# Second feed-forward product of nine of twelve tile pairs by Strassen's scheme, with a new order of all tasks

## Chip, cores and metric

One core of a Trainium2 chip runs the whole program. The metric is the device time of one execution in microseconds (us); the time of a kernel is the median of several runs. The core has five engines with a queue of their own each: TensorE (PE; its weight loads, PEld, run beside its matmuls), VectorE (DVE), ScalarE (ACT), GpSimd (POOL) and SyncE (SP), which here only issues transfers.

## The reference

```python
def _attn_ref(q, k, v, f_logit):                 # (4, 8, 768, 48) each
    f = 1.0 / (1.0 + np.exp(-f_logit))
    for t in range(S):
        state = f[:, :, t, :, None] * state + np.einsum('bhd,bhe->bhde', k[:, :, t], v[:, :, t])
        y[:, :, t] = np.einsum('bhd,bhde->bhe', q[:, :, t], state)
def _moe_ref(x, w_in, w_out):                    # x (3072, 384), w_in (384, 2048), w_out (2048, 384)
    h = x @ w_in
    g = h * (1.0 / (1.0 + np.exp(-h)))
    return (g @ w_out).astype(np.float32)
```

A gated linear attention runs over 768 steps for 4 batches of 8 heads; its output, 3072 tokens of 384, goes through a feed-forward layer with SiLU. Inputs and output are float32; the kernel multiplies in bfloat16 with sums in float32.

## The kernel before

The 768 steps of each batch are cut into six chunks of 128 tokens, so there are 24 units (batch, chunk), taken two at a time as twelve pairs `P` = 0 to 11 (`PAIRS`). Pairs 0 to 3 (form `T`) hold the first two chunks of one batch, interleaved; the others (form `N`) hold the same chunk of two batches. The two units of a pair are numbered 0 and 1.

A unit is a row of tasks, each named by its kind, its pair and more numbers. The first half is the attention: `E`, `L` (ACT: logarithm of the gate), `cs` (PE: cumulative sums), `ia`, `a`, `al` (ACT: their exponentials), `ki`, `qg` (k and q scaled, on DVE or POOL), their transpose by PE (`tq`, copied out by `qkc`) or by a transfer (`qkD`), `sc` (PE: scores), `at` (DVE: masked scores), `y`, `yi` (PE: output), `d` (PE), `sd` (DVE) and `su` (POOL or DVE) for the state, `yc`, then `yT` with `xc`, or the transfer `yD`, for the transposed output `xT`. `vb` converts v.

The second half is the feed-forward layer. `mi.P.j` (L271) multiplies two of sixteen 128-wide column blocks of `w_in` with the 256 tokens of the pair. `si.P.j` (ACT, L276) applies SiLU and leaves `hT`, the hidden values with the hidden dimension on the partitions: 16 blocks n of 128 x 256 tokens. The second product is `mo.P.i.r` (L306): for unit i, four blocks n, each one weight load of 128 x 128 from `hT` and one matmul with 384 columns of `w_out`; four such tasks sum one unit in one PSUM bank. `oc` (L185 or L187) copies the sum to `ob`, `so` (L316, L318) stores it.

Nothing is scheduled at run time. A table `PLAN` lists all tasks in one order, with the engine of each (A, V, G, S, P for ACT, DVE, POOL, SP, PE) and the buffer it takes; each engine executes its own tasks in the order of the table and waits on semaphores for what it needs. The words `idle.512.n` are n matmuls on zeros (L465) that fill PE's time at the start. PSUM has eight banks (`pb`) for everything.

Of the kernel before, what the change touches and what calls it, by code (L numbers as in the profile page):

```python
# [33 lines left out]
SLOTS = dict(f=4, k=6, q=6, v=6, e=2, lf=3, x=5, qk=5, vb=7, qkT=4, qkTT=2, atm=4, yb=3, xT=4, hT=4, sd=2, al=6, ob=6, pb=8, st0=1, st1=1, st2=1, st3=1)  # L34
# [3 lines left out]
f.2.0:S:0 k.0.0:S:0 f.0.1:S:1 f.0.0:S: E.2.0:A:0 f.1.0:S:2 L.2.0:A:0 v.1.0:S:0 q.0.0:S:0 idle.512.11::0 cs.2.1:P:0 E.0.1:A:1 E.0.0:A: k.1.0:S:1  # L38
cs.2.0:P:1 L.0.1:A:1 L.0.0:A: E.1.0:A:0 q.1.0:S:1 idle.512.1::2 cs.0.0:P:2 cs.0.1:P:3 a.0.0:A:0 vb.1.1:G:0 f.3.0:S:3 L.1.0:A:2 ia.0.1:A:1 cs.1.0:P:4
a.0.1:A:2 qg.0.0:V:0 v.0.0:S:1 cs.1.1:P:5 ia.1.0:A:3 ki.0.1:V:1 al.1:A:0 ia.0.0:A:4 qg.0.1:V: al.0:A:1 ia.1.1:A:0 k.2.0:S:2 ki.0.0:V: vb.1.0:A:1  # L40
idle.512.4::6 tq.0.1:P:6 ki.1.0:G:2 ia.2.0:A:1 tq.0.0:P:7 qkc.0.1:V:0 a.1.0:A:2 q.2.0:S:2 qkc.0.0:A: qg.1.0:V: ki.1.1:V:3 a.1.1:A:4 idle.512.3::2
tq.1.0:P:2 q.3.0:S:3 a.2.0:A:3 qg.1.1:G: sc.0.0:P:3,4 qkc.1.0:A:1 sc.0.1:P:6,7 at.0.0.1:V:0 k.3.0:S:3 wi.1:G: at.0.0.0:V: E.3.0:A:1 idle.512.2::5
tq.1.1:P:5 at.0.1.0:V:1 wi.2:G: d.1:P:1,4 qkc.1.1:A: v.2.0:S:2 su.1.0:V:0 wi.0:G: at.0.1.1:V: al.2:A:2 L.3.0:A:0 idle.512.3::2 sc.1.0:P:2,3 ki.2.0:G:4
sc.1.1:P:6,1 at.1.0.1:V:2 vb.0.0:A:2 cs.3.1:P:5 vb.0.1:A:3 at.1.1.0:V:3 qg.2.0:G: al.3:A:3 ia.2.1:A:2 d.0:P:7,3 at.1.1.1:V: a.2.1:A:0 cs.3.0:P:6
ia.3.1:A:4 su.0.0:V:0 qg.2.1:G:2 y.0:P:0,1 a.3.0:A:1 at.1.0.0:V: yc.0.0:A:0 yi.0.1:P: tq.2.0:P:7 a.3.1:A:3 wi.3:G: yc.0.1:V:1 ia.3.0:A:0 y.1:P:0,2
wo.0:G: ki.2.1:V: yc.1.0:A:2 yT.0.0:P:5 sd.0.1:V:0 yi.1.1:P: yT.0.1:P:1 yc.1.1:A:0 tq.2.1:P:6 xc.0.0:V:0 wo.1:G: xc.0.1:A: qkc.2.0:V:0 v.3.0:S:3
yT.1.0:P:0 yT.1.1:P:3 xc.1.0:A:1 mi.0.2.0:P:2 qkc.2.1:V: su.0.1:G:0 xc.1.1:A: mi.0.3.0:P:5 mi.1.3.0:P:1 sd.1.1:V:1 mi.1.3.1:P: qg.3.0:V:3 wo.2:G:
# [24 lines left out]
qg.6.1:V: al.7.1:A:5 y.5.0:P:2 qkD.6.1:S:0 a.7.1:A:0 cs.8.1:P:5 yc.5.0:A:2 tq.6.0:P:3 ia.7.1:A:3 d.6.0:P:1 qkc.6.0:V:1 vb.7.1:A:3 cs.8.0:P:2
yD.5.0:S:1 mo.4.0.1:P: ia.8.0:A:1 ki.7.1:V:4 ia.8.1:A:2 sc.6.0:P:4,3 qg.7.1:V: al.8.0:A:1 a.8.0:A:4 mo.4.0.2:P: qkD.7.0:S:2 a.8.1:A:3 at.6.0.1:V:0
# [473 lines left out]
```

## Time and profile before

| | |
|---|---|
| runs | 181.47, 181.71, 182.23 us; median 181.71 us |
| span of the profiled execution, first to last instruction | 179.2 us |
| PE matmuls, weight loads | 170.5 us busy (95%), 129.0 us (72%) |
| DVE, ACT, POOL | 79.7 us (44%), 132.7 us (74%), 61.6 us (34%) |
| DMA | 31.91 MB, 178 GB/s in the mean |

The page gives no device time of the profiled execution beside its span; the median of the runs lies 2.5 us above this span, which is taken as the time around it. Busy time is the union of the spans of an engine's instructions, and a matmul's mean duration (326 ns with 384 columns) is its latency; the rate of a run of matmuls is read from when they start. In the chain of waits a piece is the work that the end of the program waited for, with its start and its length.

### The profile page before, as it was taken

The numbers are of one execution on the slowest core, as the hardware profiler recorded it, in microseconds if no ns is written. First come the engines' busy times: TensorE is split into PE (matmuls) and PEld (weight loads), VectorE is DVE, ScalarE is ACT, GpSimd is POOL, SyncE is SP. The second block draws the span as 40 slices with busy tenths as digits, with TensorE's granted clock in tenths as the row PEclk, the third lists the DMA queues.
The fourth block names the chain that finished last, engine by engine and source line by source line (L and its number), as shares of the span: only waits on it lengthen the run. The fifth ranks groups of instructions, "written<-read, shape, count | busy, mean of one in ns | idle before, by whom it ended". The sixth has DMA issues, their size and how long they took to land.

```text
span 179.2 us, 4981 instructions
## 1 busy us (share of the span) xinstructions
PE 170.5 (95%) x2042; PEld 129.0 (72%) x2044; DVE 79.7 (44%) x166; ACT 132.7 (74%) x251; POOL 61.6 (34%) x106
## 2 busy tenths in 40 slices
PE   6769989999999999999999999999999999999993
PEld 2345779975788866778678877875876786788782
DVE  7078994008821246456673703342335747500002
ACT  3989983895289999999967558988796991178410
POOL 6036995000274004554044170636303592000010
PEclk9999999999999999999999999999999999999999
DMA  6999999999999799998478998994994496320043
GB/s 159 324 325 325 240 204 207 199 187 190 242 230 212 92 208 221 168 241 144 84 145 170 188 210 141 252 263 103 179 251 94 97 190 215 88 70 0 0 150 117
DMA packets 109366, 31.91 MB, mean 178 GB/s; under 512 B 103536, under 2 KB 108768, under 8 KB 109344
## 3 DMA queue, kind: packets, MB, share of 16 engines
q1 hardware_dynamic: 104464, 25.60, 70.2%
q0 software_dynamic: 4880, 6.00, 15.7%
q8 instruction: 16, 0.26, 0.6%
q14 instruction: 6, 0.05, 0.1%
HBM read 25.17 MB, written 4.72 MB: 167 GB/s over the span
## 4 chain that ended last, share of the span: by engine, by line
PE 77%; ACT 9%; DVE 4%; DMA 3%; SPq 2%; issue 1%; POOL 1%; DVEq 0%
PE pb L306 32%; PE pb L271 32%; ACT hT L276 4%; DMA q<-in_q_dram 3%; PE pb L373 2%; SPq L241 2%; PE pb L385 2%; PE pb L348 2%; PE pb L389 2%; DVE qk L341 2%; ACT L513 1%; DVE atm L377 1%; PE pb L331 1%; PE pb L397 1%; DVE st L420 1%
## 5 line engine op out<-in xcount | busy, mean ns | idle before, releaser
L306 PE MATMUL pb<-w_out_sb,hT 128*128 128x384 bf16 (+1 forms) x416 | 70.4, 314 | 0.2 <-ACT hT L276 0.2
L271 PE MATMUL pb<-xT,w_in_sb 128*128 128x256 bf16 (+1 forms) x672 | 68.9, 257 | 0.0
L271 PEld LDWEIGHTS <-w_in_sb 128*128 128x128 bf16 x672 | 56.6, 98 | 7.5 <-issue 0.3
L276 ACT ACTIVATE hT<-pb 128x512 bf16<-128x512 f32 x96 | 51.8, 617 | 12.4 <-PE pb L271 12.0
L306 PEld LDWEIGHTS <-hT 128*128 128x128 bf16 x416 | 37.7, 98 | 18.7 <-ACT hT L276 0.4
L377 DVE TENSOR_TENSOR atm<-pb,triu 128x512 bf16<-128x512 f32 x32 | 20.6, 684 | 20.5 <-PE pb L373 17.8
L336 ACT ACTIVATE x<-pb 128x384 f32<-128x384 f32 x48 | 22.1, 508 | 1.5 <-PE pb L331 1.4
L420 POOL TENSOR_TENSOR st<-sd,al 48x192 bf16<-48x192 f32 x32 | 16.6, 518 | 18.7 <-PE pb L385 12.1
L341 POOL TENSOR_TENSOR qk<-q,x 128x384 bf16<-128x384 f32 x11 | 11.3, 1025 | 31.9 <-ACT x L336 14.5
L513 ACT ACT_TABLE_LOAD x15 | 19.2, 1283 | 0.3
L185 ACT COPY ob<-pb 128x384 f32<-128x384 f32 (+1 forms) x15 | 6.8, 453 | 12.6 <-PE pb L306 12.6
L377 DVE TENSOR_TENSOR atm<-pb,mask 128x512 bf16<-128x512 f32 x16 | 10.2, 685 | 12.4 <-ACT hT L276 11.1
L187 DVE COPY ob<-pb 128x384 f32<-128x384 f32 (+1 forms) x11 | 5.8, 535 | 22.2 <-PE pb L306 22.2
L318 POOL DMA_DIRECT2D out_dram<-ob x8 | 4.6, 578 | 28.4 <-ACT ob L185 24.8
L316 POOL DMA_DIRECT2D out_dram<-ob x14 | 7.6, 548 | 19.6 <-DVE ob L187 15.9
L341 DVE TENSOR_TENSOR qk<-q,x 128x384 bf16<-128x384 f32 x13 | 7.6, 593 | 13.7 <-ACT x L336 13.7
L248 ACT ACTIVATE e<-f 128x768 f32<-128x768 f32 (+1 forms) x13 | 10.4, 800 | 4.4 <-DMA f<-in_f_logit_dram 4.2
L410 DVE TENSOR_TENSOR sd<-pb,st 128x384 f32<-128x384 f32 x16 | 8.9, 554 | 10.6 <-PE pb L406 3.9
L341 POOL TENSOR_TENSOR qk<-k,x 128x384 bf16<-128x384 f32 x10 | 10.8, 1082 | 6.4 <-ACT al L278 2.0
L185 ACT CAST yb<-pb 128x384 bf16<-128x384 f32 x12 | 5.6, 479 | 9.7 <-PE pb L389 9.6
L341 DVE TENSOR_TENSOR qk<-k,x 128x384 bf16<-128x384 f32 x14 | 9.9, 710 | 0.9 <-ACT x L336 0.9
L187 DVE CAST yb<-pb 128x384 bf16<-128x384 f32 x12 | 6.6, 556 | 8.0 <-PE pb L389 5.9
(72 smaller groups left out, 157.4 us busy)
## 6 DMA issues: line engine op xcount, KB each, us to landing
f<-in_f_logit_dram SPq DMA_DIRECT2D x11, 384.0 KB, 4.7
q<-in_q_dram SPq DMA_DIRECT2D x16, 192.0 KB, 4.1
v<-in_v_dram SPq DMA_DIRECT2D x16, 192.0 KB, 3.9
k<-in_k_dram SPq DMA_DIRECT2D x16, 192.0 KB, 3.9
k<-in_k_dram SPq DMA_DIRECT2D x4, 384.0 KB, 4.8
v<-in_v_dram SPq DMA_DIRECT2D x4, 384.0 KB, 9.5
q<-in_q_dram SPq DMA_DIRECT2D x4, 384.0 KB, 4.9
w_in_sb<-in_moe_w_in_dram POOLq DMA_DIRECT2D x4, 384.0 KB, 9.5
```

The source lines that it names most:

```text
L185: nc.scalar.copy(dst, src)
L187: ENG[eng].tensor_copy(dst, src)
L248: return nc.scalar.activation(e, at("f", P)[:, j * w:(j + 1) * w], AF.Exp, scale=-1.0)
L271: nc.tensor.matmul(h[:, i, cols], w_in_sb[:, kk, n * 128:(n + 1) * 128], at("xT", P)[:, kk, cols], start=(kk == 0), stop=(kk == KT - 1))
L276: return nc.scalar.activation(at("hT", P)[:, 2 * j:2 * j + 2, :], at("h", P, j).rearrange("p (n c) -> p n c", n=2), AF.Silu)
L306: nc.tensor.matmul(at("o", P, i)[:, cols], at("hT", P)[:, n, i * C:(i + 1) * C], w_out_sb[:, n, cols], start=(n == 0), stop=(n == NT - 1))
L336: nc.scalar.activation(at(kind, P, i).rearrange("p h d -> p (h d)"), at("cs", P, i)[:, 0:HD], AF.Exp, scale=1.0 if kind == "ia" else -1.0)
L341: ENG[eng].tensor_mul(at("qk", P, i)[:, j, :, 0:D], heads("qk"[j], P, i), at("ia" if j else "a", P, i))
L377: ENG[eng].tensor_mul(at("atm", P, i)[:, r], at(f"s{r}", P, i).rearrange("p (n c) -> p n c", c=C), mask[:, None, :].to_broadcast([C, NP, C]))
L410: nc.vector.tensor_add(at("sd", P, i), d_ps, prev_state(P, i))
L420: ENG[eng].tensor_mul(at("st", P, i)[lo:lo + D, :, r * D:(r + 1) * D], src[lo:lo + D, :, r * D:(r + 1) * D], al_of(P, i)[lo:lo + D, :, Non ...
L513: nc.scalar.preload_act_table_set(TABLES[mode])
```

## The change

For pairs 2 to 10 the second product is done in blocks. Let A be the 256 tokens x 2048 hidden values, cut into the two units u and two halves k of the hidden dimension (eight blocks n each), and B be `w_out`, cut into two halves r of its rows and two halves c of its columns. In place of 32 matmuls with 384 columns there are seven products `ms.P.1` to `ms.P.7` of eight matmuls with 192 columns each:

M1 = (A00+A11)(B00+B11), M2 = (A10+A11)B00, M3 = A00(B01-B11), M4 = A11(B10-B00), M5 = (A00+A01)B11, M6 = (A10-A00)(B00+B01), M7 = (A01-A11)(B10+B11).

The sums of B are made once by five instructions `wt` on DVE. The sums of A are made for each pair by four instructions `hs` on DVE, bfloat16 in and out: `hs.P.5` with 2048 elements to a partition into a buffer of class `qkTT`, `hs.P.1` with 1024 into one of class `qkT`, `hs.P.6` and `hs.P.7` with 1024 in place in `hT`. One bank (`oa`) sums M3, M5 in one half and M4, M2 in the other. After M3 and M4 alone, `cc` (copy) and `ca.P.0` (DVE) take them into a buffer `ct`; only then may M2 and M5 be added in that bank. `ca.P.1` adds M1, `ca.P.2` and `ca.P.3` form the two diagonal blocks of the output and `oc.P` copies the two others. All of `ca` is on DVE.

`hT` gets the order (unit, n, token), the output buffer holds both units, E writes over `f`, and there are fewer buffers for f, k, q, v and `ob`. Pairs 0, 1 and 11 keep `mo`. The table is another one throughout: the pairs start in the order 1, 0, 2, 3 in place of 2, 0, 1, 3, there are 33 `idle` matmuls in place of 24, twelve `tq` in place of ten, and 25 of the store instructions are issued by SP in place of 12.

```diff
-SLOTS = dict(f=4, k=6, q=6, v=6, e=2, lf=3, x=5, qk=5, vb=7, qkT=4, qkTT=2, atm=4, yb=3, xT=4, hT=4, sd=2, al=6, ob=6, pb=8, st0=1, ...)
+SLOTS = dict(f=3, k=5, q=5, v=5, lf=3, x=5, qk=5, vb=7, qkT=5, qkTT=2, atm=4, yb=3, xT=4, hT=4, sd=2, al=6, ob=3, pb=8, st0=1, ..., ct=2)
...
-f.2.0:S:0 k.0.0:S:0 f.0.1:S:1 f.0.0:S: E.2.0:A:0 f.1.0:S:2 L.2.0:A:0 v.1.0:S:0 q.0.0:S:0 idle.512.11::0 cs.2.1:P:0 E.0.1:A:1 E.0.0:A: k.1.0:S:1
+f.1.0:S:0 q.1.0:S:0 f.0.0:S:1 f.0.1:S: f.2.0:S:2 k.1.0:S:0 E.1.0:A: L.1.0:A:0 E.0.0:A: f.3.0:S:0 idle.512.7::0 cs.1.0:P:0 ia.1.0:A:0 k.0.0:S:1
...
+    KH, W = NT // 2, d_model // 2
+    w_sum = {m: sb.tile([128, KH, W], BF16, name=f"w_sum{m}") for m in (1, 3, 4, 6, 7)}
...
+    BANK = {2: "oa", 3: "oa", 4: "oa", 5: "oa", 6: "ob2", 7: "ob2", 1: "oc"}
+    def h_sum(P, m):
+        if m == 5:
+            return at("hE", P).rearrange("p i j n g c -> p (i j n g c)").rearrange("p (u n c) -> p u n c", u=2, c=C)
+        if m == 1:
+            return at("hF", P).rearrange("p j n c -> p (j n) c")
+        return at("hT", P)[:, 1, 0:KH, :] if m == 6 else at("hT", P)[:, 0, KH:NT, :]
...
+        if kind == "wt":
+            blk = lambda r, c: w_out_sb[:, r * KH:(r + 1) * KH, c * W:(c + 1) * W]
+            x, y, op = {1: (blk(0, 0), blk(1, 1), ALU.add), 3: (blk(0, 1), blk(1, 1), ALU.subtract), ...}[rest[0]]
+            return ENG[eng].tensor_tensor(out=w_sum[rest[0]], in0=x, in1=y, op=op)
...
+        if kind == "hs":
+            x, y, op = {6: (blk(1, 0), blk(0, 0), ALU.subtract), 7: (blk(0, 1), blk(1, 1), ALU.subtract), 1: (blk(0, 0), blk(1, 1), ALU.add),
+                        5: (hT[:, :, 0:KH, :], hT[:, :, KH:NT, :], ALU.add)}[m]
+            return ENG[eng].tensor_tensor(out=h_sum(P, m), in0=x, in1=y, op=op)
+        if kind == "ms":
+            for n in range(KH):
...
+                half = 1 if m in (2, 4, 6) else 0
+                first = n == 0 and m in (1, 3, 6, 7)
+                nc.tensor.matmul(at(BANK[m], P)[:, half * W:(half + 1) * W], x, w, start=first, stop=(n == KH - 1), skip_group_check=True)
+            return
+        if kind == "cc":
+            return copy(eng, at("ct", P), at("oa", P)[:, W:2 * W])
+        if kind == "ca":
+            if rest[1] < 2:
+                return nc.vector.tensor_add(ct, at("oa", P)[:, 0:W] if rest[1] == 0 else at("oc", P)[:, 0:W], ct)
+            diag = at("ob", P).rearrange("p u (x w) -> p (u x) w", w=W)[:, 0:4:3, :]
+            if rest[1] == 2:
+                return nc.vector.tensor_sub(diag, ct[:, None, :].to_broadcast([C, 2, W]), two(at("oa", P)))
+            return nc.vector.tensor_add(diag, two(at("ob2", P)), diag)
...
-                e = at("e", P)[:, j * w:(j + 1) * w]
+                e = at("f", P)[:, j * w:(j + 1) * w]
...
-            return nc.scalar.activation(at("hT", P)[:, 2 * j:2 * j + 2, :], at("h", P, j).rearrange("p (n c) -> p n c", n=2), AF.Silu)
+            return nc.scalar.activation(at("hT", P).rearrange("p u n c -> p n u c")[:, 2 * j:2 * j + 2], at("h", P, j).rearrange("p (n u c) -> p n u c", n=2, u=2), AF.Silu)
...
-                nc.tensor.matmul(at("o", P, i)[:, cols], at("hT", P)[:, n, i * C:(i + 1) * C], w_out_sb[:, n, cols], start=(n == 0), stop=(n == NT - 1))
+                nc.tensor.matmul(at("o", P, i)[:, cols], at("hT", P)[:, i, n], w_out_sb[:, n, cols], start=(n == 0), stop=(n == NT - 1))
```

What the change moves is shown at three places, each engine's instructions in their order, with the numbers of the buffers behind the names. In PE's program, before, late in the kernel: the end of a task of the second product (384 columns to a matmul), then the first product of the next pair.

```order
3898 L306 MATMUL pb_140<-w_out_sb,hT_125 128x384
3899 L306 LDWEIGHTS hT_125
3900 L306 MATMUL pb_140<-w_out_sb,hT_125 128x384
3901 L271 LDWEIGHTS w_in_sb
3902 L271 MATMUL pb_141<-xT_121,w_in_sb 128x256
```

PE's program now, near its end: the end of M5 of pair 10 (the sum of A, in buffer `qkTT_104`, as the weights, 192 columns of `w_out_sb`), then half a task of pair 11 by the old way.

```order
4488 L273 MATMUL pb_135<-w_out_sb,qkTT_104 128x192
4489 L273 LDWEIGHTS qkTT_104
4490 L273 MATMUL pb_135<-w_out_sb,qkTT_104 128x192
4491 L370 LDWEIGHTS hT_120
4492 L370 MATMUL pb_134<-w_out_sb,hT_120 128x192
```

Each matmul keeps a weight load of its own, and there are more and narrower ones. In DVE's program in the middle of the kernel, before: masked scores (L377), state sums (L410), scaled q and k (L341).

```order
92 L410 TENSOR_TENSOR sd_127<-pb_140,st_151 128x384
93 L377 TENSOR_TENSOR atm_113<-pb_146,triu 128x512
94 L187 CAST yb_116<-pb_146 128x384
95 L341 TENSOR_TENSOR qk_96<-k_70,x_90 128x8x48
96 L377 TENSOR_TENSOR atm_114<-pb_143,triu 128x512
97 L377 TENSOR_TENSOR atm_114<-pb_141,triu 128x512
98 L341 TENSOR_TENSOR qk_94<-q_71,x_92 128x8x48
```

DVE's program now, at a like place: between the same kinds stand the assembly of pair 3 (L284, L285) and the sums of A of pair 4 (L256), with two operands in SBUF.

```order
120 L284 TENSOR_TENSOR ob_129<-ct_145,pb_134 128x2x192
121 L193 CAST yb_111<-pb_137 128x384
122 L285 TENSOR_TENSOR ob_129<-pb_133,ob_129 128x2x192
123 L193 COPY xT_115<-pb_139 128x3x128
124 L442 TENSOR_TENSOR atm_108<-pb_132,triu 128x512
125 L442 TENSOR_TENSOR atm_108<-pb_133,triu 128x512
126 L256 TENSOR_TENSOR qkT_101<-hT_118 128x1024
127 L193 CAST vb_94<-v_77 128x384
128 L256 TENSOR_TENSOR qkTT_104<-hT_118 128x2048
129 L442 TENSOR_TENSOR atm_109<-pb_138,triu 128x512
```

Scores that stood close together now wait behind sums of up to 2048 elements. DVE's end, before: the last masked scores, then only copies of sums to the output buffer.

```order
153 L377 TENSOR_TENSOR atm_114<-pb_145,triu 128x512
154 L377 TENSOR_TENSOR atm_113<-pb_146,triu 128x512
155 L187 COPY ob_134<-pb_142 128x384
156 L187 CAST yb_116<-pb_144 128x384
157 L187 COPY ob_139<-pb_145 128x384
158 L187 COPY ob_137<-pb_140 128x384
159 L187 COPY ob_134<-pb_146 128x192
```

DVE's end now: the sums of A and the assembly of pair 10 (`ct_144`, `hT_117`), with the copies of pair 11 (`ob_130`) between.

```order
223 L281 TENSOR_TENSOR ct_144<-pb_135,ct_144 128x192
224 L256 TENSOR_TENSOR hT_117<-hT_117 128x1024
225 L193 COPY ob_130<-pb_136 128x192
226 L281 TENSOR_TENSOR ct_144<-pb_132,ct_144 128x192
227 L193 COPY ob_131<-pb_135 128x384
228 L284 TENSOR_TENSOR ob_131<-ct_144,pb_135 128x2x192
229 L285 TENSOR_TENSOR ob_131<-pb_137,ob_131 128x2x192
230 L193 COPY ob_130<-pb_134 128x192
```

The last two additions of pair 10 stand ahead of DVE's last copy.

More of the change, by code (lines that the diff above doesn't have):

```diff
@@ L40 @@
[L40 to L47, printed above, removed]
@@ L425, in takes @@
     def takes(kind, rest):
-        if kind in ("wi", "wo", "so", "yi", "idle"):
+        if kind in ("wi", "wo", "wt", "so", "yi", "yj", "idle"):
             return []
```

209 lines of the change are left out of this document (131 added, 78 removed).

## Prediction

> **What bounds the kernel now.** I read the page's busy times and slices first, to see whether one engine is full:
>
> ```profile
> span 179.2 us, 4981 instructions
> PE 170.5 (95%) x2042; PEld 129.0 (72%) x2044; DVE 79.7 (44%) x166; ACT 132.7 (74%) x251; POOL 61.6 (34%) x106
> PE   6769989999999999999999999999999999999993
> PEclk9999999999999999999999999999999999999999
> GB/s 159 324 325 325 240 204 207 199 187 190 242 230 212 92 208 221 168 241 144 84 145 170 188 210 141 252 263 103 179 251 94 97 190 215 88 70 0 0 150 117
> ```
>
> then the busy time by stretches (PE, PEld, DVE, ACT, POOL with counts, granted clock, DMA):
>
> ```profile
> 0.00:27.00 27.00, 21.69 (x360) 13.94 (x362) 18.72 (x54) 22.76 (x45) 16.29 (x35) 1.00 1.09 263
> 27.00:176.00 149.00, 148.66 (x1688) 115.09 (x1682) 60.98 (x112) 109.64 (x205) 45.28 (x72) 1.00 0.84 164
> 176.00:179.20 3.20, 0.17 (x3) 0.00 (x0) 0.00 (x0) 0.32 (x1) 0.00 (x0) 1.00 0.36 123
> ```
>
> From 27 to 176 us PE is busy for 148.66 of 149.00 us at full clock. What it executes there is paid one to one; DVE is free for 59% of it. Ahead lies a start of 27 us that loads and small tasks set, behind it 3 us of copy and store. Busy PE is not yet PE at its rate, so the third view is the chain of waits, for runs of one kind, and the timeline of the end:
>
> ```profile
> 149.54 0.65 PE pb L306 x4
> 35.00 0.67 PE pb L271 x12
> 34.55 0.45 PE pb L348 x8
> 25.87 0.85 issue
> 174.69 1.48 PE L306 MATMUL pb<-w_out_sb,hT 128*128 128x192 bf16 x16
> L306 PE MATMUL pb<-w_out_sb,hT 128*128 128x192 bf16 x64 | 6.3, 246 | 0.0
> ```
>
> Four matmuls with 384 columns take 0.65 us, 162 ns each. The last sixteen have 192 columns: 1.48 us less the 0.246 us latency of the last, over 15, is 82 ns each. So the cost goes with the columns, with only some 2 ns for a narrower instruction.
>
> **The change, part by part.** *Products.* Nine pairs lose 32 matmuls each: 288 x 0.65/4 = 46.8 us. They get 56 each: 504 x 0.082 = 41.3 us. PE saves 5.5 us, all in the stretch where it is full.
>
> Each of the 504 needs a weight load. The chain shows 12 matmuls of 128 columns (the halves of pairs 0 and 1) in 0.67 us, 56 ns each with a load each, so a load hides under far less than 82 ns. [...]
>
> *Transposes.* Two more units go by `tq` on PE: 2 x 0.45 = 0.9 us added. Net: -4.6 us.
>
> *Instruction fetches.* PE gets 24 more matmuls and loads to a pair, 4572 instructions for 4090.
>
> ```profile
> q8 instruction: 16, 0.26, 0.6%
> ```
>
> Sixteen fetches bring 0.26 MB, one for 256 PE instructions; the changed program needs 18. Of the sixteen only one shows as a wait, the 0.85 us of "issue" at 25.87, in a burst of score matmuls while the loads keep DMA full. A Strassen product is slow to consume instructions (82 ns for two), so the two new fetches cost nothing while PE is in the product. Bounds: the new order avoids the wait (-0.85) or meets two of them (+0.85). I take -0.4, the middle.
>
> *Start.* Before its first product with `w_in` PE now has 35 tasks in place of 28: the transposes of pair 3, scores and state of pair 2, sums of pair 4. They are only drawn forward, so what counts is PE's empty time.
>
> ```profile
> 1.37 4.37 PE L465 MATMUL pb<-zero,triu 128*128 128x512 bf16 x11 [1.37 <-POOL triu masks.py:66]
> 23.58 1.84 PE L271 MATMUL pb<-xT,w_in_sb 128*128 128x128 bf16 x30
> f<-in_f_logit_dram SPq DMA_DIRECT2D x11, 384.0 KB, 4.7
> ```
>
> Eleven fillers take 4.37 us (0.40 each, at half clock); the first run is now 7, so -1.6. Later fillers rise from 13 to 26; a filler of 512 columns costs 4/3 of 162 ns at full clock, 0.216, so +2.8 if none fills time that was empty anyhow. Of the empty PE time in the first 27 us (27.00 - 21.69 = 5.3) 1.37 lies ahead of the first filler, so some 4 us could be filled, and the net lies between -1.6 and +1.2. On the other side 17 loads of 384 KB in place of 14 stand ahead of the first piece of `w_in`, 1.2 MB more at the 325 GB/s of the page's slices, 3.6 us later on the wire, while the first use lies at 23.58 us and is drawn back by some 3 us of tasks. I take +0.3, with -1.6 and +2.5 as ends.
>
> *DVE.* This is what the change adds outside PE. The rows:
>
> ```profile
> L377 DVE TENSOR_TENSOR atm<-pb,triu 128x512 bf16<-128x512 f32 x32 | 20.6, 684 | 20.5 <-PE pb L373 17.8 <-ACT hT L276 2.6
> L187 DVE COPY ob<-pb 128x384 f32<-128x384 f32 x10 | 5.4, 552 | 22.0 <-PE pb L306 22.0
> L187 DVE COPY ob<-pb 128x192 f32<-128x192 f32 x1 | 0.4, 359 | 0.2 <-PE pb L306 0.2
> L187 DVE COPY qkTT<-pb 128x1024 bf16<-128x1024 bf16 x3 | 2.0, 680 | 0.0
> L187 DVE COPY xT<-pb 128x384 bf16<-128x384 bf16 x4 | 1.4, 353 | 4.8 <-PE pb L397 4.8
> L187 DVE CAST vb<-v 128x384 bf16<-128x384 f32 x11 | 5.1, 482 | 0.0
> ```
>
> No row has a sum of two bfloat16 operands. By the two bfloat16 copies an element costs (680-353)/640 = 0.51 ns, by the two float32 copies (552-359)/192 = 1.01 ns. That bounds a sum of 1024 elements by 0.68 and 1.20 us, one of 2048 by 1.20 and 2.23, one of 1536 by 0.94 and 1.71. I take the lower ends, since the type is that of the bfloat16 rows. New on DVE: 9 x 1.20 + 27 x 0.68 (`hs`), 5 x 0.94 (`wt`), 18 x 0.36 and 18 x 0.55 (`ca`), 4 x 0.36 (`cc`): 51.7 us. The rest of its work shrinks by some 6.5: nine fewer `qk` products (0.65 each, rows below), six fewer `vb` (0.48), three fewer `ob` and one `yb` (0.55), against six more `xT` (0.35), three more `qkT` (0.68) and a half-width `ob` (0.36). DVE goes to 125 us of some 175.
>
> What it delays is queued behind it: masked scores, `yc`, state. From the first `hs` to the end the order gives PE 113 us by these rows and DVE 95, but not evenly: cut into stretches of 8 us of PE work, five of fourteen hold 8.2 to 8.6 us of DVE instructions for 8.1 to 8.4 of PE. DVE instructions overlap by some 0.08 us (one every 0.48 us with 0.55 us of length, below), so that is 90% full. PE will wait there now and then. M2 and M5 add another wait: PE may not touch bank `oa` until `cc` and `ca.P.0` have read it; other tasks stand between. Bounds for all of it: 0, where the order leaves enough between, and 4.5 us, 0.9 in each of the five. I take +1.3, nearer to the lower end since DVE has 18 us to spare over the whole.
>
> *Edits at no cost.* ACT loses six `xT` and six `ob` copies and gains five `cc`; it is 74% busy. The stores that go from POOL to SP are hidden by loads that run far ahead. At the end 28 matmuls of pair 11 (28 x 0.082 = 2.3 us) follow M6 of pair 10 and cover its two last additions (2 x 0.55); without that cover they would add 1.1 us.
>
> *Sum.* 179.2 - 5.5 + 0.9 - 0.4 + 0.3 + 1.3 = 175.8 us of span; with the 2.5 us between this span and the median of the runs, 178.3 us.
>
> **Rivals.** *DVE and POOL block each other.* POOL's products, and DVE's with two SBUF operands, in one stretch of both timelines:
>
> ```profile
> 139.96 0.56 DVE L341 TENSOR_TENSOR qk<-q,x 128x384 bf16<-128x384 f32 x1 [3.05 <-ACT x L336]
> 140.44 0.55 DVE L410 TENSOR_TENSOR sd<-pb,st 128x384 f32<-128x384 f32 x1
> 141.64 1.35 DVE L341 TENSOR_TENSOR qk<-k,x 128x384 bf16<-128x384 f32 x1
> 141.20 1.37 POOL L341 TENSOR_TENSOR qk<-k,x 128x384 bf16<-128x384 f32 x1 [1.85 <-issue]
> L341 DVE TENSOR_TENSOR qk<-k,x 128x384 bf16<-128x384 f32 x14 | 9.9, 710 | 0.9 <-ACT x L336 0.9
> L341 DVE TENSOR_TENSOR qk<-q,x 128x384 bf16<-128x384 f32 x13 | 7.6, 593 | 13.7 <-ACT x L336 13.7
> ```
>
> Undisturbed such a DVE product takes 0.55 us; beside POOL's one took 1.35. Over the 27 of them 14 x 0.16 + 13 x 0.043 = 2.8 us are lost, 0.10 each. Now there are 59 (36 `hs`, 5 `wt`, 18 `qk`), 3 us more lost, several in each full stretch, and each up to 0.8 us at once, with the scores behind it. If that takes the slack of the five stretches, PE loses 0.5 to 1 us more in each: 181 to 183.5 us, 182 in the middle. Against it: the lost time fits into DVE's 18 us, and in this trace PE did not stop for such a collision. [...]
>
> *Sums at one element a cycle: slower than before.* Were the upper ends true, DVE would get 9 x 1.03 + 27 x 0.52 + 5 x 0.77 = 27 us more, and from the first `hs` to the end 120 us for PE's 113. DVE is then the bound; the point is 113. The excess of 7 us replaces the 1.3, and loose fits add to it: 184 to 188 us, 186 taken. The bfloat16 copy rows speak against it.
>
> *Weight loads at their full length: slower.* A mean load lasts 98 ns:
>
> ```profile
> L306 PEld LDWEIGHTS <-hT 128*128 128x128 bf16 x416 | 37.7, 98 | 18.7 <-ACT hT L276 0.4
> ```
>
> If each 192-column product took that, 504 x 0.098 = 49.4 us, 2.6 more than now in place of 5.5 fewer: 186.4 us. [...] The sixteen matmuls at 82 ns all but exclude it.
>
> *A late start.* If the first product comes 3 us later, by data or fetches, 181 us.
>
> *All of it goes well.* No DVE wait, the fetch wait gone, the start 1 us shorter: 179.2 - 4.6 - 0.85 - 1 + 2.5 = 175.3 us.
>
> **How the numbers follow.** Forecast 0.58, with 176.5 to 180.6 as its own range; all goes well 0.11; blocking 0.15; late start 0.06; slow sums 0.08; weight loads 0.02. The predicted time is the forecast's, 178.3. From 175.3 to 183 the range leaves out half of "all goes well" (0.05), the top of blocking (0.04) and the two slow cases (0.10). Changes under 0.5% (0.9 us) a measurement of this kernel hardly tells from none: faster means below 180.8, slower above 182.6. Faster: 0.57 of the forecast, 0.11, 0.03 of blocking and late start: 0.71. Blocking is half "same", with the rest of late start and forecast 0.12. Slower: 0.06 of blocking, 0.01 of the late start, 0.08, 0.02: 0.17.
>
> **What the changed profile would show.** Eight matmuls of L273 in some 0.66 us, with no idle time of PE by weight loads: the first term. Sums of 1024 elements on DVE near 0.68 us, not 1.20. Waits of PE for DVE (masked scores, sums, `ct`) that add up to 1 to 2 us after 27 us, and at most one fetch wait. The first product with `w_in` at 23 to 27 us. The prediction is wrong if PE's idle time in the middle exceeds 4 us, if DVE's sums run at 1 ns an element, or if the product matmuls come slower than 90 ns apart.

## The result, and the profile after

The changed kernel takes 188.49 us in the median of five runs (187.31 to 191.51); the kernel before, timed beside it, 181.56. The ratio is 1.0389, 95% interval 1.0332 to 1.0446: 3.9% slower. 178.3 us was forecast, in a range that ended at 183.0: the direction was wrong. The ratios here leave out runs more than 1.5% above a kernel's fastest; since most orders made from the changed one scatter by 2 to 6.6 us, where the kernel before scatters by 1 to 2.4, the median of all runs stands beside each ratio.

The page of the changed kernel, its span, busy times and slices (the profiled execution took 187.31 us, 1.9 more than its span):

```profile
span 185.4 us, 5567 instructions
PE 171.1 (92%) x2284; PEld 145.3 (78%) x2285; DVE 121.3 (65%) x238; ACT 131.8 (71%) x245; POOL 68.4 (37%) x108
PE   6799979899993999999999979999999899999992
PEclk9999999999999699999999999999999999999999
GB/s 160 322 324 293 241 237 204 200 184 159 200 133 71 201 161 209 144 216 195 171 214 131 169 221 184 140 170 188 213 146 152 184 37 143 73 0 4 68 191 129
```

The row of PE has holes: a 3 in the thirteenth slice (near 56 us), where the DMA moves only 71 GB/s, and in the slice after it the clock is down. The stretches (columns as before):

```profile
0.00:27.00 27.00, 23.16 (x345) 13.76 (x346) 17.53 (x51) 22.02 (x44) 16.00 (x34) 1.00 1.04 265
27.00:182.00 155.00, 147.86 (x1941) 131.54 (x1939) 103.78 (x188) 109.50 (x202) 52.43 (x75) 0.99 0.81 154
60.30:63.60 3.30, 3.30 (x19) 1.74 (x19) 0.00 (x0) 3.27 (x6) 0.00 (x0) 0.50 1.08 211
```

From 27 us on PE is empty for 155.00 - 147.86 = 7.1 us, where it was empty for 0.34. The third row is the stretch behind the largest hole: 3.3 us at half clock, worth 1.65 us of work at full clock. Now the operations that the sum of the prediction priced: two pieces of the chain of waits (first product, `w_out` product), and DVE's sums by shape (least/median/longest ns):

```profile
66.53 0.66 PE pb L273 x8
65.88 0.65 PE pb L370 x4
L256 DVE TENSOR_TENSOR qkTT<-hT x9: 1215/1216/1526, 64.7 to 168.0; 128x2048 bf16<-128x2048 bf16 x9
L256 DVE TENSOR_TENSOR hT<-hT x18: 674/682/1029, 70.2 to 174.3; 128x1024 bf16<-128x1024 bf16 x18
L246 DVE TENSOR_TENSOR w_sum<-w_out_sb x5: 941/950/957, 52.7 to 71.5; 128x1536 bf16<-128x1536 bf16 x5
```

All of them cost what was forecast. What TensorE waits for is new (`issue` stands for a wait whose end nothing in the profile explains):

```profile
PE pb L467 <- ACT hT L340: 3.1, 1, 3.1
PE pb L438 <- DMA qkT<-qk: 2.3, 2, 1.6
PE pb L349 <- issue: 0.6, 1, 0.6
PE pb L361 <- issue: 0.4, 1, 0.4
```

None of these rows is a wait for one of DVE's new sums. The first is `yT.4.1`, which waits for a bank that a SiLU on ACT has to free. The chain leads back to a load of f. ACT's timeline shows the SiLU's place in the queue, behind the exponential of pair 6, two logarithms and a load of a function table; SP's rows show why the slice is empty of transfers:

```profile
41.06 13.01 DMA f<-in_f_logit_dram
54.09 0.84 ACT L312 ACTIVATE f<-f 128x768 f32<-128x768 f32 x1 [3.53 <-DMA f<-in_f_logit_dram]
54.97 1.58 ACT L327 ACTIVATE lf<-f 128x768 bf16<-128x768 f32 x2
56.56 1.28 ACT L593 ACT_TABLE_LOAD   x1
57.86 2.56 ACT L340 ACTIVATE hT<-pb 128x512 bf16<-128x512 f32 x5
44.09 3.62 SPq L305 DMA_DIRECT2D q<-in_q_dram  x1
56.90 1.34 SPq L424 DMA_TRANSPOSE qkT<-qk  x1
```

From 47.7 to 56.9 us SP issues nothing: the transposing transfer of pair 4 stands at its head and waits for POOL's product with q, which itself waits for the load of q until 55.62 us. The wait for f isn't the same in every execution: among the orders that leave pair 6's exponential in its place, ACT waits 3.5 us for f here, 2.6 in the profiled run of `stores_pool`, 1.6 in that of `old_product`, and not at all in those of `no_sums`, `fill_hole` and `shift_only`, none of which moves that load. The 2.3 us are two scores (`sc.8.1`, `sc.11.1`) that wait for their transposes at 109 and 147 us. And the first product with `w_in` comes at 29.47 us instead of 23.58:

```profile
29.47 0.94 PE L335 MATMUL pb<-xT,w_in_sb 128*128 128x128 bf16 x14
```

In sum: PE ends 5.9 us later although it has 4.6 less to do, 10.5 us in all. Of these 6.8 are empty time behind 27 us (7.14 - 0.34), 1.65 the half clock. The rest, 2.1, is what is left over and is put down to the start.

### The profile page after: what moved, and what is told of

The parts are those of the page before. It is cut to its first block, busy times and chain, and to the rows that moved or that the text cites. A ratio compares the mean times of both kernels' runs of the same rounds, so it can differ in the third digit from the quotient of the medians.

```text
span 185.4 us, 5567 instructions
## 1 busy us (share of the span) xinstructions
PE 171.1 (92%) x2284; PEld 145.3 (78%) x2285; DVE 121.3 (65%) x238; ACT 131.8 (71%) x245; POOL 68.4 (37%) x108
## 4 chain that ended last, share of the span: by engine, by line
PE 52%; DMA 22%; SPq 6%; POOL 6%; ACT 5%; issue 4%; DVE 2%; POOLq 0%; DVEq 0%
PE pb L335 22%; PE pb L273 15%; DMA f<-in_f_logit_dram 9%; PE pb L370 7%; DMA qkT<-qk 6%; SPq L305 5%; POOL qk L405 3%; DMA v<-in_v_dram 3%; DMA k<-in_k_dram 2%; PE pb L438 2%; DMA q<-in_q_dram 2%; ACT hT L340 1%; POOL w_in_sb L237 1%; PE pb L459 1%; PE pb L455 1%
## 5 line engine op out<-in xcount | busy, mean ns | idle before, releaser
L340 ACT ACTIVATE hT<-pb 128x512 bf16<-128x512 f32 x96 | 51.2, 607 | 20.7 <-PE pb L335 20.4
L273 PE MATMUL pb<-w_sum,hT 128*128 128x192 bf16 x288 | 28.2, 246 | 0.0
L405 POOL TENSOR_TENSOR qk<-k,x 128x384 bf16<-128x384 f32 x15 | 15.4, 1029 | 23.0 <-DMA k<-in_k_dram 13.0
L370 PE MATMUL pb<-w_out_sb,hT 128*128 128x384 bf16 (+1 forms) x128 | 19.1, 292 | 0.0
L312 ACT ACTIVATE f<-f 128x768 f32<-128x768 f32 (+1 forms) x13 | 10.2, 795 | 6.4 <-DMA f<-in_f_logit_dram 6.3
L273 PE MATMUL pb<-w_out_sb,qkTT 128*128 128x192 bf16 x144 | 14.5, 246 | 0.0
L256 DVE TENSOR_TENSOR hT<-hT 128x1024 bf16<-128x1024 bf16 x18 | 12.9, 719 | 0.0
L273 PEld LDWEIGHTS <-qkTT 128*128 128x128 bf16 x144 | 11.9, 98 | 0.3
L545 PE MATMUL pb<-zero,triu 128*128 128x512 bf16 x32 | 10.6, 460 | 1.4 <-POOL triu masks.py:66 1.4
L256 DVE TENSOR_TENSOR qkTT<-hT 128x2048 bf16<-128x2048 bf16 x9 | 11.3, 1251 | 0.0
L281 DVE TENSOR_TENSOR ct<-pb,ct 128x192 f32<-128x192 f32 x18 | 6.3, 352 | 7.0 <-ACT hT L340 3.2
```

The costliest lines, as they stand in the source:

```text
L256: return ENG[eng].tensor_tensor(out=h_sum(P, m), in0=x, in1=y, op=op)
L273: nc.tensor.matmul(at(BANK[m], P)[:, half * W:(half + 1) * W], x, w, start=first, stop=(n == KH - 1), skip_group_check=True)
L312: return nc.scalar.activation(e, at("f", P)[:, j * w:(j + 1) * w], AF.Exp, scale=-1.0)
L340: return nc.scalar.activation(at("hT", P).rearrange("p u n c -> p n u c")[:, 2 * j:2 * j + 2], at("h", P, j).rearrange("p (n u c) -> p n u ...
L370: nc.tensor.matmul(at("o", P, i)[:, cols], at("hT", P)[:, i, n], w_out_sb[:, n, cols], start=(n == 0), stop=(n == NT - 1))
L405: ENG[eng].tensor_mul(at("qk", P, i)[:, j, :, 0:D], heads("qk"[j], P, i), at("ia" if j else "a", P, i))
```

## Experiments

All are edits of the changed kernel unless said otherwise. In the diffs a word of `PLAN` is `task:engine:buffer`; (+) and (-) mark where it stands now and stood.

**The product by itself: old product, no sums, and both without late loads.** In `old_product` the places of M1 to M7 hold 32 matmuls of 384 columns, four or six to a place:

```diff
-            for n in range(KH):
+            N = 4
+            N += 2 if m in (6, 7) else 0
+            for n in range(N):
...
+                nc.tensor.matmul(at(BANK[m], P)[:, 0:2 * W], x, w_out_sb[:, n], start=(n == 0 and m in (1, 3, 6)), stop=(n == N - 1), skip_group_check=True)
```

> The changed order, its sums and its evictions stay, but TensorE does in the places of the nine pairs' seven products 32 matmuls of 384 columns instead of 56 of 192 (four for products 1 to 5, six for 6 and 7); the output is not the reference's. Theory (the product itself saves what 504 x 82 ns against 288 x 162 ns say, 5.3 us, and the loss lies in the order): 188.4 + 5 = 193.5 us, between 192.5 and 194.5. Rival (the product saves nothing where TensorE waits for loads anyway): 188 to 190 us.

Measured: 190.48 us (187.63 to 194.19), ratio to the kernel before 1.0399 (1.0353 to 1.0445). Only 2.0 us over the changed kernel, by the ratio nothing: in this order most of the product's gain isn't to be had. That TensorE then only meets its next wait at another time is argued here; the runs without late loads below bear on it. `no_sums` drops the 36 words `hs` (the products read blocks of `hT`):

> The 36 sums of hidden blocks are left out (29 us of VectorE); the products read the blocks themselves, and the output is not the reference's. Theory (VectorE at 65% busy is not what TensorE waits for; loads and the start are): 187 to 188.2 us, at most 1.5 us less. Rival (VectorE's longer queue delays products q times a, transposes and evictions, and so everything): 182 to 184.5 us.

189.25 us, 1.0415 (1.0387 to 1.0442): no faster, and over both forecasts, although DVE has 28 us less to do. TensorE's waits for the transposed q and k grow instead, in its list of waits:

```profile
PE pb L438 <- DMA qkT<-qk: 4.8, 4, 1.7
```

So VectorE isn't what holds the kernel. `dense` and `dense_old` leave out the loads of q, k, v of pairs 5 to 11. They also have pair 6's gate behind the SiLUs and the load k.3.0 earlier, two moves that come below:

```diff
-        emit(kind, rest, eng)
+        kind in "kqv" and rest[0] >= 5 or emit(kind, rest, eng)
```

> Loads of q, k and v of pairs 5 to 11 are left out (8 MB; the products read what older pairs left in the buffers, and the output is not the reference's); E.6.0 stands behind the silus and k.3.0 one row earlier. Theory (late loads are the loss behind 35 us): TensorE idles under 1.5 us behind the first w_in product, 188.4 - 3.3 - 1.6 - 3.3 = 180 us, between 178 and 182. Rival (the order itself, or VectorE and ACT, hold TensorE): 184 us or more.

> As the run without loads of pairs 5 to 11, with 32 matmuls of 384 columns for 56 of 192 in the nine pairs (the output is not the reference's). Theory (with TensorE dense the product is worth what its matmuls say): 5 us more than the run without loads, between 4 and 5.5. Rival (the product is worth little: in the changed order the old product cost 1 to 2 us only): 0 to 2 us more.

`dense`: 183.16 us (180.46 to 186.6), 1.0000 (0.9961 to 1.0038). `dense_old`: 187.84, 1.0331 (1.0290 to 1.0372). The medians stand 4.7 us apart, the ratios 3.3% (6 us). With TensorE nearly full the product is worth its matmuls:

```profile
35.00:175.00 140.00, 138.19 (x1775) 124.61 (x1773) 99.95 (x176) 102.91 (x188) 50.11 (x69) 1.00 0.49 99
```

That is `dense` from 35 to 175 us, in an execution of 180.60 us, one of its fastest: PE empty for 1.8 us of 140, with all of VectorE's sums in place. `dense`'s own forecast (178 to 182) was missed by 1.2 us in the median. By the ratio it only equals the kernel before, although the late loads are gone: its first product with `w_in` still comes at 29.5 us instead of 23.58.

**Loads: one late f, a hole, pair 4, buffers.** `late_e6` moves pair 6's gate behind the SiLUs:

```diff
-E.6.0:A: ... L.6.0:A:2 ... si.3.4:A:3 ... cs.6.0:P:5 ... si.3.2:A: ... f.8.0:S:1 cs.6.1:P:1 ... L.7.0:A:1
+si.3.4:A:3 ... si.3.2:A: ... E.6.0:A: L.6.0:A:2 cs.6.0:P:5 cs.6.1:P:1 f.8.0:S:1 L.7.0:A:1
```

> The exponential and the logarithm of pair 6 (E.6.0, L.6.0) stand behind the silus of pairs 2 and 3 on ACT instead of ahead of them, with the sums over time of pair 6 (cs.6) and the load f.8.0 behind them; no load comes earlier. Theory (a late load of f holds ACT's queue, and TensorE with it): the 3.3 us of idle TensorE between the fourth product block of pair 0 at 54.6 us and yT.4.1 at 58.5 us go, and the half clock behind it, worth 1.6 us: 188.4 - 4.5 = 183.9 us, between 183 and 185.5. Rival (all loads are late, TensorE only meets the next one): under 1.5 us less, 187 to 188.4 us.

188.79 us (186.31 to 191.08), 1.0272 (1.0245 to 1.0299), in the median over both forecasts. The stall at 54 us is gone from its trace, and a shorter one, 1.6 us at 64 us for pair 6's logarithm, stands in its place. By the ratio 1.2% are won, by the median nothing: in the profiled run k of pair 3 landed late, POOL and then TensorE stood in the start, and TensorE ran at half clock for 6.8 us behind it. POOL's timeline in the changed kernel, and there:

```profile
24.85 1.01 POOL L405 TENSOR_TENSOR qk<-k,x 128x384 bf16<-128x384 f32 x1
27.98 0.99 POOL L405 TENSOR_TENSOR qk<-k,x 128x384 bf16<-128x384 f32 x1 [2.64 <-DMA k<-in_k_dram]
```

`fill_hole` moves one word:

```diff
-qkD.4.0:S:1 ... q.5.1:S:0 k.5.0:S:0 k.6.0:S:1 k.5.1:S: q.6.0:S:1
+q.5.1:S:0 k.5.0:S:0 k.6.0:S:1 k.5.1:S: q.6.0:S:1 qkD.4.0:S:1
```

> One row of SP's queue moves: the transposing DMA of pair 4 (qkD.4.0), for which SP stands still from 47.7 to 56.9 us while the DMA share falls to three tenths, goes behind the five loads of q and k of pairs 5 and 6 that followed it. Theory (the DMA engines are the scarce thing up to 140 us, and what is lost in that hole comes back as late loads at 109, 126 and 147 us): the hole fills, those waits (3.1 us together) shrink by half or more, the stall at 54 us stays: 185.5 to 187.3 us. Rival (later loads are bound by buffers and SP's issuing, not by the hole): 188 to 189 us.

186.83 us, 1.0263 (1.0216 to 1.0311): 1.7 us less, as the theory had it. In its trace the waits for transposes at 109 and 147 us are down to 0.2 us, but a wait of 2.0 us for an exponential on ACT, which ends at 125.5 us, is new, with half clock behind it. The stall at 54 us is gone too, which the theory hadn't; the edit can't be the direct reason, since f of pair 6 is issued ahead of the moved word. `dense4` is `dense` without pair 4's loads as well:

> As the run without loads of pairs 5 to 11, with the loads of pair 4 left out too (1.2 MB between 21 and 47 us; the output is not the reference's). Theory A (the DMA engines are full up to 40 us, and pair 4's loads delay the weights and each other): the first w_in product 1 to 2 us earlier than at 29.5 us, no wait for qk or qkT between 35 and 62 us, and little spread: 179 to 180.5 us. Theory B (the start hangs on POOL's chain of casts and products from 17.5 to 29 us): the first w_in product stays within 0.5 us of 29.5; only the waits behind it go: 181 to 182.5 us.

181.53 us, 0.9986 (0.9961 to 1.0011); the first product with `w_in` came at 30.37 us. That is no earlier than with these loads, so theory A is out and B is nearer, though it had the first product within 0.5 us of 29.5: pair 4's loads are not what delays the start. Behind it they cost 1.6 us by the medians, but only 0.3 by the ratios, whose intervals overlap. `before_few` gives the kernel before the smaller numbers of buffers (`f=3, k=5, q=5, v=5`):

> The kernel before with the changed kernel's number of buffers: three for f instead of four, five each for k, q and v instead of six; its order stays, and loads wait for the buffer instead. Theory (fewer buffers shorten the lead of the loads): 0.5 to 2.5 us more, 182.1 to 184.1 us, with waits for loads in the second half. Rival (the order of SP's queue sets the lead, not the buffers): 181.3 to 182 us.

181.39 us, 0.9998 (0.9977 to 1.0019). The theory fell: the buffers that the change gave up cost nothing in the old order. That a load's time is set by its place in SP's queue instead is the rival's reading; this run doesn't show it by itself.

**Stores on SP.** `stores_pool` issues on POOL what the change had moved to SP (thirteen instructions by count, not the fourteen of the text below):

```diff
-so.0.0:S: so.0.1:S: so.1.0:S: so.1.1:S: so.2.0:S: so.2.1:S: so.4.1:S:
+so.0.0:G: so.0.1:G: so.1.0:G: so.1.1:G: so.2.0:G: so.2.1:G: so.4.1:G:
```

> The fourteen store instructions that the change issues on SP between 82 and 142 us (units of pairs 0 to 2 and the second unit of pair 4) are issued on POOL again, at the same places of the plan. Theory (SP's issuing is the resource: from 80 to 150 us its issues take 64 of 70 us, and loads and transposes stand behind stores): some 8 us of issuing leave SP, and the waits for transposes at 109 and at 147 us (1.8 and 0.8 us) shrink: 186 to 187.5 us. Rival (the loads start late because buffers come free late, whoever issues): 188 to 188.8 us. Rival (POOL's own queue then holds its products q times a): slower, 189 to 190 us.

185.59 us, 1.0198 (1.0156 to 1.0241): 2.9 us less, more than forecast. `before_stores_sp` makes the opposite edit in the kernel before:

> The kernel before, with the same stores moved from POOL to SP as the change moves (units of pairs 0 to 2, second unit of pair 4), at their own places. Theory (SP's in-order issuing delays loads wherever they have little lead): its loads lead by 10 to 40 us, so 0 to 1 us more: 181.6 to 182.6 us. Rival (stores on SP cost what they gave back in the changed kernel, 2.9 us, whatever the lead): 183.5 to 185 us.

183.83 us, 1.0105 (1.0067 to 1.0143): 2.3 us more, so again the rival was right and not the lead of the loads. SP's queue in the kernel before, and the same place with the stores in it:

```profile
103.43 1.27 SPq L360 DMA_TRANSPOSE qkT<-qk  x1
104.74 3.36 SPq L401 DMA_TRANSPOSE xT<-yb  x2
108.21 1.78 SPq L360 DMA_TRANSPOSE qkT<-qk  x1
```

```profile
104.20 1.66 SPq L360 DMA_TRANSPOSE qkT<-qk  x1
105.90 1.70 SPq L316 DMA_DIRECT2D out_dram<-ob  x2
107.64 4.03 SPq L401 DMA_TRANSPOSE xT<-yb  x2
111.78 1.24 SPq L360 DMA_TRANSPOSE qkT<-qk  x1
```

SP isn't free there: a store of a unit (two instructions here) takes 1.1 to 2.7 us of its time, and each transpose behind it starts later by that and by the stores before, 3.6 us in the last row. In the kernel before, loads of q and k behind 60 us are issued 4.4 to 38.6 us ahead of their first use (12.7 in the median for q, 10.4 for k). Its transposes of q and k are issued 4.7 to 9.9 us ahead of their scores and land 3.0 to 5.3 us after the issue. With the stores in the queue TensorE's list of waits has transposes, where the kernel before has no wait for a transfer behind 20 us:

```profile
PE pb L373 <- DMA qkT<-qk: 1.5, 1, 1.5
PE pb L271 <- DMA xT<-yb: 1.2, 2, 0.9
```

The opposite is seen in `stores_pool`, where the row of 2.3 us of the changed kernel is down to this:

```profile
PE pb L438 <- DMA qkT<-qk: 0.2, 1, 0.2
```

**Together.** `combo1` has `stores_pool`, `fill_hole`, `late_e6`, and k.3.0 ahead of q.3.0; `combo2` four moves more:

> Four moves together: stores back on POOL, the transpose of pair 4 behind five loads, pair 6's exponential and logarithm behind the silus, and the load k.3.0 one row earlier (ahead of q.3.0; it landed at 24.9 us in one run and at 28.0 us in another, with POOL and TensorE waiting). Theory (these waits are the loss and they add up): 185.6 with the stores alone, less 2.5 for the stall at 54 us, 1 for the hole and 0.7 for the start: 181.4 us, between 180 and 183. Rival (a wait that goes is replaced by the next): 184 to 186 us.

> The four moves of combo1, and four more for the waits left in its trace (1.6 us for tq.4.1 at 39 us, whose loads took 14 us to land; 1.4 us for the transpose of pair 4 at 60 us; POOL without a pause from 17.5 to 30 us): q.4.0 issued ahead of f.6.0, tq.4.1 four blocks of products later, the first part of w_out issued behind ki.4.1, and two casts of v of pair 0 on ACT instead of POOL. Theory (each wait is a late load or a full queue, and none is behind it): 183.6 less 1.2, 1.0 and 0.5: 180.9 us, between 180 and 182, under the kernel before. Rival (what is moved makes others late by as much): 183 to 184.5 us.

183.56 us, 1.0106 (1.0070 to 1.0142), and 183.49, 1.0116 (1.0082 to 1.0150): the first between its two forecasts, the second where its rival had it. What `combo2` won at 39 us its profiled run lost in the start, in a wait of 1.6 us without a releaser (`issue`) in the middle of `d.2`.

**Fetches.** `combo3` keeps the better of these moves; `combo3s` and `combo3t` add small matmuls that do nothing:

```diff
-idle.512.9::2 cs.2.0:P:2
+idle.512.9::2 idle.16.19::2 cs.2.0:P:2
```

> combo1 with the moves of combo2 that its trace bore out (q.4.0 ahead of f.6.0, tq.4.1 four blocks later, the first part of w_out later), the two casts left on POOL, the transpose of pair 4 behind three loads instead of five, and its reader sc.4.0 two blocks of products later. Theory (waits for pair 4's data at 39 us and 60 us, 1.6 and 1.5 us in combo1, vanish, and the start is combo1's): 183.6 - 2.7 = 180.9 us, between 180.2 and 182. Rival (the start moves by 2 us with chance, as in combo2, and eats it): 182.5 to 183.5 us.

> combo3 with 19 matmuls of 16 columns (38 instructions, 0.5 us, in TensorE's idle time at 10 us) that do nothing but move every later instruction within the blocks that TensorE fetches: waits without a releaser stood at the instructions 416, 700 and 956 of every trace of the changed order, 256 to 284 apart, at the tenth matmul or so of a burst of small ones. Theory (these are late fetches): the waits stand at the same count of instructions, so 38 earlier in the program: that in d.2 falls into the transposes ahead of it, where TensorE waits 0.4 us for VectorE anyway; 0.3 to 1.2 us less than combo3. Rival (the wait belongs to d.2 itself, as for a value or a bank): it stays in d.2, same time or up to 0.3 us more.

> combo3 with 45 such matmuls (90 instructions, 1.1 us, 0.7 us more than the idle time there). Theory of fetches: the wait of d.2 moves into sc.2.1, another burst of small matmuls, and stays as long: 0.3 to 1 us more than combo3. Rival: it stays in d.2, 0.7 us more than combo3; where the wait stands in the trace tells the two apart, not the time.

`combo3`: 183.46 us (181.21 to 185.54), 1.0067 (1.0030 to 1.0104): as the rival said, the start ate it. `combo3s`: 181.45 (181.03 to 183.37, ten of twelve below 181.7), 1.0004 (0.9973 to 1.0034). `combo3t`: 183.17 (181.43 to 186.12), 1.0061 (1.0027 to 1.0095), by its time no better than `combo3`. PE's timeline at `d.2` in `combo3`, with a stretch of its page behind it, and then at `d.2` in `combo3s`:

```profile
27.04 0.35 PE L361 MATMUL pb<-vb,qk 64*128 64x96 bf16 x5
28.86 0.41 PE L361 MATMUL pb<-vb,qk 64*128 64x96 bf16 x11 [1.47 <-issue]
```

```profile
30.00:33.60 3.60, 3.60 (x41) 3.43 (x37) 1.80 (x4) 3.23 (x8) 0.00 (x0) 0.53 1.24 212
```

```profile
28.23 0.52 PE L361 MATMUL pb<-vb,qk 64*128 64x96 bf16 x16 [0.31 <-POOL vb L193]
```

`combo3` stops for 1.47 us inside sixteen equal matmuls and then runs for 3.6 us at a clock of 0.53; a shift of 38 instructions takes both away. So the wait isn't `d.2`'s own. Where such waits stand in the traces speaks for the fetch. In thirteen of the twenty traces, the kernel before among them, a wait of over 0.2 us without a releaser ends at the 703rd to 705th of TensorE's recorded matmuls and weight loads, at the 960th or 961st, or at both, two places 256 apart, whatever task stands there (at 26.72 us in the kernel before, at 27.97 and 34.44 in the changed one); packets of the queue `q8 instruction` start 2.2 to 2.6 us before it ends. (The place near 416 that the text above names has a releaser, DVE, and not every trace has the other two.) None of the traces with shifted instructions has such a wait. In `combo3t` it is gone from `d.2` too, but not found in `sc.2.1`, where the theory had put it: shown is that such a wait goes with the place among TensorE's instructions, not a rule for where the next one falls. The changed kernel's 18 packets of `q8 instruction` for 4572 instructions are one for 254, near the distance of 256 between the two places. That the waits are late fetches is the author's reading of these figures; by it a fetch cost 1.47 us in `combo3`. The same edit alone in the changed kernel, `shift_only`:

> The changed kernel with nothing but the 19 small matmuls of combo3s at 10 us. Theory (the waits without a releaser in d.2 and y.2, 0.4 and 0.6 us in its profile and up to 1.5 us with a half clock behind it in others, are late fetches, and they cost 0.5 to 2 us by run): 186.5 to 188 us against 188.5, and the two waits gone from the trace. Rival (in this order other waits at 54, 109 and 147 us swallow what the start gains): 188 to 189 us, the waits gone all the same.

185.33 us (183.18 to 186.29), 1.0173 (1.0124 to 1.0221): 3.2 us less, more than the theory allowed. Both waits, 1.0 us together, are gone from its trace. So is ACT's wait for f of pair 6, which the edit doesn't touch, so not all of the 3.2 us can be put down to the fetch.

**The mended order, with either product.** `combo4` moves the tasks around the two longest waits of `combo3s` between 40 and 62 us (0.4 and 1.0 us in its trace); `combo4_old` has the old product in it:

> combo3s with its two largest waits answered: the block mi.0.7.0 stands two blocks later (it waited 0.6 us for its bank at 41 us), and the fourth block of the second unit of pair 0 stands ahead of cs.6.0 (1.1 us at 60 us). Theory: 181.5 less 0.6 and 0.6: 180.3 us, between 179.8 and 181, under the kernel before (181.5). Rival (another wait takes their place): 181.2 to 182 us.

> combo4 with 32 matmuls of 384 columns for 56 of 192 in the nine pairs (the output is not the reference's; all loads stay). Theory (in an order without waits the product is worth what its matmuls say, 5 us, as without loads it was 4.7): 4.5 to 5.5 us over combo4. Rival (with the loads in place waits swallow part of it, as in the changed order, where it was 2 us): 2 to 4 us.

`combo4`: 182.02 us, 1.0027 (1.0002 to 1.0053): as the rival said, no gain; its trace has other waits (0.6 us for a bank and 1.0 for transposes). `combo4_old`: 186.92, 1.0300 (1.0274 to 1.0326): 4.9 us more. With all loads in place and most of the order's waits gone the product gives its 5 us. No version tried that computes the whole output beats the kernel before; `combo3s` equals it within 0.3%.

## Why the prediction was wrong, point by point

*Products, -5.5: right.* 0.66 us for eight, and 4.9 us (`combo4_old`) and 4.7 us (`dense_old`) when taken back. The rival of full-length weight loads is out: 98 ns loads stand behind matmuls that start 82 ns apart.

*Sums on VectorE at the lower ends: right,* 0.68, 1.22 and 0.95 us. *VectorE's lateness, +1.3: about nothing;* without 28 us of its work the kernel was no faster, and `dense` keeps TensorE nearly full with all of its sums. Both rivals built on VectorE are out.

*Fetches, -0.4: the wrong sign, and too small a bound.* The step priced a late fetch at the one wait seen (0.85 us) and let two of them be the worst case. In the profiled run of the changed kernel two waits came, 1.0 us together, so 0.2 more than before. In other executions of this order the first alone took up to 1.6 us (`combo2`), and half clock for 3.4 us followed. Taking it away gave 2.0 us by the medians and 1.1 by the ratios (`combo3` to `combo3s`); `shift_only`'s 3.2 us hold more than the fetch.

*Start, +0.3: 2.1 us in the profiled run, as what is left over,* near its upper end of 2.5. The first `w_in` product comes at 29.0 to 33.2 us over the runs, where 23 to 27 was forecast; the rival of a late start, priced at 3 us, came in part. A late k (2.64 us for POOL in the run of `late_e6`) is part of it where it comes late; pair 4's loads, of those that the step added at 3.6 us on the wire, are not (`dense4`). Which of POOL's and ACT's tasks hold the rest of the start is open: moving two casts off POOL (`combo2`, with three more moves) brought nothing that could be told from the start's own scatter.

*"Edits at no cost": the step that failed.* "The stores that go from POOL to SP are hidden by loads that run far ahead" looked at the loads. SP issues in order (in the changed kernel nothing from 47.7 to 56.9 us, behind one transfer that waits) and in the kernel before is issuing for some 28 of the 30 us from 100 to 130 us, and the transposes of q and k in the same queue have little lead to give (4.7 to 9.9 us from issue to use, of which 3.0 to 5.3 go to the landing). A term put at nothing cost 2.3 us in the old order and 2.9 in the new.

*What was not a term at all, and cost the most in the profiled run:* two places where a queue stands behind one late transfer, ACT behind f of pair 6 (3.1 us of TensorE, and 1.65 by the half clock behind it) and SP behind q of pair 4. The first doesn't come in every execution. The prediction counted each engine's work but didn't go through SP's and ACT's queues for what stands behind a wait. Its wrong-if line (over 4 us empty in the middle) is what came: 7.1 us. And the time around the span was 1.9 us, not 2.5.

The three edits that were timed alone with effect, stores, hole and fetches, gave 2.9, 1.7 and 3.2 us, 7.8 in sum (9.7 by the ratios); `combo3s`, which holds them all (the transpose of pair 4 behind three loads in place of five) and six moves more, is 7.0 us under the changed kernel by either. So what they give overlaps.

## What to carry to other kernels

Where TensorE is full, a saving in matmuls is real and only shows if the order around it has no waits (4.7 and 4.9 us here in the orders with few of them, 2.0 in the changed one): price the order as a change of its own, queue by queue. On an in-order queue that issues transfers look at the row with the least lead, not at the most, and count the issuing time of every row put ahead of it; at each wait ask what stands behind it on the same engine. And where a wait without a releaser sits in a burst of small matmuls, try a shift of the instructions by a few idle ones before redesigning the order, and time it: 38 instructions gave 2.0 us here by the medians (`combo3s`), 90 gave 0.3 (`combo3t`).

## What the runs showed of the hardware

A hole can cost twice: after 3.1 us of waiting, up to 58.5 us, TensorE ran 3.3 us at a clock of 0.50. In these traces the granted clock changes only in steps of 3.41 us: in the changed kernel it is full for 51.2 us from 8.96 us on, half for 3.41 and full for 122.9. In the 3.41 us ahead of four of the steps at half clock TensorE was busy for 41 to 57% of the time: for 1.50 us in the changed kernel, 1.94 in `combo3` (with a single wait of 1.47 us), 1.68 in `shift_only` and 1.40 in `fill_hole`. The busy time alone doesn't tell when such a step comes: in `stores_pool` 1.64 busy us, from 57.76 us on, were followed by the full clock. The half rate of the first fillers shows in their starts: in the kernel before they are 427 ns apart up to 4.76 us, and 217 behind 5.15 us.

In the first 50 us of the changed kernel, where the mean busy share of the DMA reads 1.09, a load's time from issue to landing isn't a constant. One of f, of 384 KB, issued at 41.06 us, took 13.0 us, where the median of these loads is 5.6. The load of k of pair 3 had landed by 24.85 us, when POOL took it up, in the profiled run of the changed kernel, and at 27.98 in that of `late_e6`, whose order is the same up to there. That is one source of the scatter of these orders; how much of it, and why the old order has less, is not shown.
